# When the second weight slice is fetched and converted, in an attention-then-SwiGLU kernel

## The chip, the core and the metric

One NeuronCore of one Trainium2 chip. The metric is device time in microseconds (us) of one execution. TensorE (PE) multiplies, VectorE (DVE) and ScalarE (ACT) do the elementwise work, and SyncE (SP) issues nearly all DMAs, one after the other in program order.

## The reference

Attention over 4 batches, 12 heads, 448 positions, head size 64, with a sigmoid in place of the softmax, and then a gated feed-forward layer on the 1792 x 768 result:

```python
scores = scale * np.matmul(q, k.transpose(0, 1, 3, 2)) - np.log(S)
attn = 1.0 / (1.0 + np.exp(-scores))
x = np.matmul(attn, v)                       # (4, 12, 448, 64) -> (1792, 768)
xn = x / np.sqrt(np.mean(x * x, axis=-1, keepdims=True) + 1e-06) * rms_g
g = xn @ w_gate                              # 768 x 1536
out = (g * (1.0 / (1.0 + np.exp(-g))) * (xn @ w_val)) @ w_out
```

## The kernel before, in words

The attention runs in 12 units u of four heads; a batch is three units. A unit has 7 steps c. A step is 12 fp16 score matmuls (`scores`, L282, into `sc`), one sigmoid on ACT over 128 x 896 (L286, into one of four `a_b` buffers), and 8 fp32 matmuls with v (`av`, L297). Each fp32 operand of the fp16 products is cut into a high and a low fp16 half.

The loop over `n` (0, 2, ..., 84; called slot n here) walks the 84 steps in pairs: slot n does the scores of steps n and n+1 and then `av` of steps n-2 and n-1. Step 7u + c is step c of unit u, so unit 5 begins at step 35, whose scores are in slot 34 and whose `av` is the second one of slot 36. Unit 6 begins at step 42: scores in slot 42, `av` first in slot 44. Unit 7 begins at step 49 (scores second in slot 48, `av` second in slot 50).

What feeds a unit, in the order of the steps (the table `FILL`, L853): at steps c = 0 to 3 of unit u, DVE splits k and q of unit u+2 (`qk_hi` L227, `qk_lo` L231); behind the last of these, SP issues one transpose DMA (`transpose_both` L234, `xc<-room`) for unit u+2. At c = 4 SP loads k and q of unit u+4. When unit u's last `av` is issued, SP loads v of unit u+2 (`load_v`) into the buffer that unit u has left; there are two v buffers, and a v load is two DMAs of 224 KB. Below, T(u), kq(u) and v(u) are the transpose and the loads of unit u.

Batch results are normalised (`norm`, L340): PE sums squares (`ssq`), DVE computes the inverse root on small tiles, PE spreads it to a row (`rinv`, L392), ACT copies that (L393), DVE scales (L396), adds and subtracts (L403, L418), and the fp16 halves are made (L400 on ACT for batches 0 and 3, L407 on DVE).

The feed-forward layer multiplies by slices of w_gate and w_val of 256 columns each (two-level Strassen products, hence the differences between blocks). A slice of one kind is loaded by three DMAs (`load_w`, L459: one of 384 KB, two of 192 KB) that are put into the list `loads` and go out when `run_load` is called. It is then converted: three DVE steps undo the packing (`to_f32`, L444 to L446), four DVE subtractions form block differences (L496), and ACT and DVE cut the result into fp16 halves (L499, L502). `split_w` returns these steps in two lists: `first` begins with four entries for the gate half (a step that flushes due loads, and the three of `to_f32`, the last of which also puts the next slice's transfers into `loads`), then four for the value half, then the differences; `second` holds the fp16 halves. For slices 0 and 1 the gate and value halves are separate entries.

The steps are not issued at once. `run_later` (L805) is called after every `scores` and every `av`; each call gives a credit of 0.8 for DVE (at most 2.5) and 0.18 for ACT, and takes entries from `adds`, then `norms`, then `splits` as long as the credit is above zero, charging each its cost; `wait` entries let a call pass. The k/q splits are charged too. So what stands in `splits`, and from which slot on, sets where in DVE's in-order stream the other entries come. `SPLIT_AT`, `REST_AT` and `LOADS_AT` (L71, L72) are the slots at whose end entries are put into `splits` and loads are issued. Before the change slice 1's transfers go out one at the end of slot 18, one at 20, two at 26 and two at 28, and all its conversion is put into `splits` at the end of slot 30.

Of the kernel before, what the change touches and what calls it, by code (L numbers as in the profile page):

```python
# [24 lines left out]
def attention_then_swiglu(  # L25
# [42 lines left out]
    ps_m = ctx.enter_context(tc.tile_pool(name="ps_m", bufs=4, space=bass.MemoryType.PSUM))  # L68

    WARM = 5  # L70
    SPLIT_AT, REST_AT = (8, 30), 12  # L71
    LOADS_AT = {18: 1, 20: 1, 26: 2, 28: 2}  # L72
    NAT = (0, 2, 0, 1, 2, 0, 1, 2, 0, 1, 0, 1)
    PIECES = (0, 4), (4, 3)
    K_PIECES = (0, 2), (2, 3), (5, 2)
# [136 lines left out]
    def g_columns():  # L212
        ps = bank("g")
        nc.tensor.matmul(ps[:, :NCC], g_row, ident[:NCC, :NCC], start=True, stop=True)
        nc.vector.tensor_copy(g_sb.rearrange("p (c o) -> p o c", o=2), ps[:, :NCC].rearrange("p (o c) -> p o c", o=2))
# [55 lines left out]
    def scores(u, c):  # L271

        T = t_b[u % 3]
        ps = banks("sc")

        for n, (l, m) in enumerate(PARTS):
            for r in range(2):
                rows = slice(D * r, D * r + D)
                for j in range(2):
                    cols = slice(PB * j, PB * j + PB)  # L280
                    o = ps[cols, r, :S].rearrange("p (c x) -> p c x", c=NSLOT)
                    nc.tensor.matmul(  # L282
                        o, T[rows, 1, l, c, cols], T[rows, 0, m, :, cols], start=(n == 0), stop=(n == 2)
                    )
        a = at[u, c] = a_b[(u * NSLOT + c) % 4]
        nc.scalar.activation(  # L286
            a, ps[:, :, :S], AF.Sigmoid, bias=-math.log(S), scale=1.0 / (math.sqrt(D) * SQ * SQ)
        )

    def av(u, c):  # L290
        a = at.pop((u, c))
        if c == 0:
            pav[u] = [bank("av") for _ in range(2)]
        for r, ps in enumerate(pav[u]):
            for j in range(2):
                rows = slice(PB * j, PB * j + PB)
                nc.tensor.matmul(  # L297
                    ps[D * (j ^ r) : D * (j ^ r) + D, :S],
                    v_b[u % 2][rows, r, c],
                    a[rows, r],  # L300
                    start=(c == 0),
                    stop=(c == NSLOT - 1),
                )
        if c == NSLOT - 1:
            for r, ps in enumerate(pav.pop(u)):
                evict(u, r, ps)
            if u + 2 < NU:
                load_v(u + 2)
# [21 lines left out]
    def run_evictions(n):  # L330
        for part in evictions[:n]:
            part()
        del evictions[:n]
# [132 lines left out]
    def run_load():  # L466
        if loads:
            loads.pop(0)[1]()
# [331 lines left out]
    adds, norms, splits = [], [], []  # L800
# [4 lines left out]
    def run_later():  # L805
        calls[0] += 1
        credit[0] = min(credit[0] + SLOT, 2.5)
        credit[1] = min(credit[1] + ACT_SLOT, 0.6)
        for queue in (adds, norms, splits):
            while queue:  # L810
                part, cost, *on_act = queue[0]
                if part is wait:
                    if cost <= calls[0]:
                        queue.pop(0)
                    break
                if credit[bool(on_act)] <= 0:
                    break
                queue.pop(0)
                part()
                credit[bool(on_act)] -= cost  # L820
# [49 lines left out]
    with tc.manual_schedule():  # L870
# [28 lines left out]
        split = {}  # L899
        for n in range(0, len(todo) + 2, 2):  # L900
            for u, c in todo[n : n + 2]:
                scores(u, c)
                run_evictions(1)
                for part in FILL[c]:
                    part(u)
                if n == 6 and c == 6:
                    g_columns()
                run_later()
            for u, c in todo[max(n - 2, 0) : n]:
                av(u, c)  # L910
                run_evictions(1)
                run_later()
            for _ in range(LOADS_AT.get(n, 0)):
                run_load()
            if n in SPLIT_AT:
                fc = SPLIT_AT.index(n)
                split[fc] = split_w(fc)
                first, second = split[fc]
                splits.extend(first[:4] if fc == 0 else first + second)
            if n == REST_AT:  # L920
                splits.extend(split[0][0][4:] + split[0][1])
        run_evictions(len(evictions))


# [46 lines left out]
        for fc, n in order:  # L971
# [5 lines left out]
            elif fc + 1 < NFC:  # L977
                first, second = split[fc + 1] = split_w(fc + 1) if n == 0 else split[fc + 1]
# [97 lines left out]
```

## Time and profile before

| what | value |
|---|---|
| runs of the kernel | 579.77, 578.42, 576.60 us; median 578.42 |
| the profiled execution | 577.24 us, of which the span is 575.4 |
| PE busy | 562.7 us (98%) |
| DVE busy | 437.9 us (76%) |
| ACT busy | 265.7 us (46%) |
| attention | from the first scores at 8.10 us to about 140 us; then PE works on the feed-forward layer without a gap to the end |

A span row of PE is a share of modelled matmul time; the stretches in which PE has no work are read from the timeline. The timeline merges neighbouring instructions of one kind into a row; in brackets stands the idle time of the engine before the row and what ended it.

### The profile page before, as it was taken

How to read it: one execution, taken by the hardware profiler on the slowest of the kernel's cores; microseconds unless marked ns; L12 is line 12 of the kernel's file. 1: busy time of each engine (PE TensorE's matmuls, PEld its weight loads, DVE VectorE, ACT ScalarE, POOL GpSimd, SP SyncE). 2: the span in 40 equal slices, each digit the busy share in tenths (PEclk: the TensorE clock that was granted, in tenths of full speed). 3: DMA queues.
4: the chain of work that ended last, by engine and by line, in shares of the span. 5: the costliest groups of instructions: out<-in, count | busy, mean ns of one | idle time of the engine just before them, and what ended most of it. 6: DMA issues, size and time to landing. Idle time of an engine off the chain costs nothing.

```text
span 575.4 us, 10231 instructions
## 1 busy us (share of the span) xinstructions
PE 562.7 (98%) x4224; PEld 306.1 (53%) x4224; DVE 437.9 (76%) x577; ACT 265.7 (46%) x398; POOL 0.7 (0%) x6
## 2 busy tenths in 40 slices
PE   8999979999999999999999999999999999999997
PEld 6555435454555555555555555555556566666664
DVE  4897499998887777878778787787557987777751
ACT  5788778887454243342433424334438342222220
POOL 0000000000000000000000000000000000000000
PEclk9999999999999999999999999999999999999999
DMA  8999998972016356282662825732526576444211
GB/s 260 253 217 261 222 255 202 222 168 41 1 43 173 117 158 197 88 227 68 168 190 96 220 78 158 191 104 66 179 59 224 152 224 188 149 145 146 69 41 42
DMA packets 99201, 87.25 MB, mean 152 GB/s; under 512 B 38735, under 2 KB 92242, under 8 KB 99154
## 3 DMA queue, kind: packets, MB, share of 16 engines
q1 hardware_dynamic: 98594, 85.91, 56.7%
q8 instruction: 33, 0.54, 0.4%
q10 hardware_dynamic: 560, 0.69, 0.3%
q14 instruction: 14, 0.11, 0.1%
HBM read 61.34 MB, written 16.52 MB: 135 GB/s over the span
## 4 chain that ended last, share of the span: by engine, by line
PE 90%; DVE 5%; DMA 2%; ACT 1%; issue 1%; SPq 0%; DVEq 0%; ACTq 0%
PE cb L532 28%; PE cd L532 14%; PE av L297 7%; PE oc L735 7%; PE od L735 7%; PE o L735 7%; PE ca L532 7%; PE sc L282 6%; PE ob L735 4%; DMA wr<-in_moe_w_val_dram 1%; DVE room L231 1%; DVE room L396 1%; DVE room L322 1%; ACT room L286 1%; PE tr L251 1%
## 5 line engine op out<-in xcount | busy, mean ns | idle before, releaser
L532 PEld LDWEIGHTS <-wr 128*128 128x128 f16 x1512 | 147.9, 98 | 138.6 <-issue 1.0
L532 PE MATMUL cb<-xc,wr 128*128 128x448 f16 x756 | 147.3, 352 | 0.0
L286 ACT ACTIVATE room<-sc 128x896 f32<-128x896 f32 x84 | 75.1, 930 | 19.5 <-PE sc L282 18.8
L297 PE MATMUL av<-room 64*64 64x448 f32 x672 | 73.7, 538 | 1.4 <-DMA room<-in_v_dram 1.4
L532 PE MATMUL cd<-xc,wr 128*128 128x448 f16 x324 | 65.2, 352 | 0.0
L282 PE MATMUL sc<-xc 64*64 64x448 f16 x1008 | 59.8, 351 | 4.9 <-ACT room L286 4.2
L282 PEld LDWEIGHTS <-xc 64*64 64x64 f16 x1008 | 32.2, 106 | 34.9 <-issue 24.2
L587 DVE TENSOR_TENSOR room<-cd,room 128x448 f32<-128x448 f32 x24 | 15.0, 625 | 43.1 <-PE cd L532 43.1
L735 PEld LDWEIGHTS <-xc 128*128 128x128 f16 x360 | 35.2, 98 | 23.3
L502 DVE SCALAR_TENSOR_TENSOR wr<-wr 128x1536 f16<-128x1536 f32 (+3 forms) x28 | 37.3, 1355 | 10.7 <-ACT wr L499 10.7
L532 PE MATMUL ca<-xc,wr 128*128 128x448 f16 x216 | 44.8, 352 | 0.0
L735 PE MATMUL o<-room,wr 128*128 128x384 f16 x252 | 41.1, 326 | 0.0
L297 PEld LDWEIGHTS av<-room 64*64 64x64 f32 x672 | 27.1, 133 | 24.2 <-issue 16.8
L555 ACT ACTIVATE room<-cb 128x448 f32<-128x448 f32 x24 | 13.0, 543 | 53.8 <-PE cb L532 53.8
L576 ACT ACTIVATE room<-cb 128x448 f32<-128x448 f32 x24 | 13.0, 543 | 50.6 <-PE cb L532 30.6
L735 PEld LDWEIGHTS <-room 128*128 128x128 f16 x270 | 26.4, 98 | 17.5
L499 ACT ACTIVATE wr<-wr 128x768 f16<-128x768 f32 (+1 forms) x48 | 33.9, 758 | 0.0
L590 ACT ACTIVATE room<-room 128x448 f32<-128x448 f32 x24 | 13.8, 577 | 43.2 <-DVE room L587 43.2
L735 PEld LDWEIGHTS <-wr 128*128 128x128 f16 x252 | 24.7, 98 | 16.3
L690 ACT ACTIVATE xc<-xc 128x1536 f16<-128x1536 f32 (+1 forms) x12 | 14.5, 1259 | 35.7 <-DVE xc L687 35.7
L496 DVE TENSOR_TENSOR wr<-wr 128x384 f32<-128x384 f32 x48 | 26.5, 553 | 0.8
L548 ACT ACTIVATE room<-cb 128x448 f32<-128x448 f32 x24 | 13.0, 544 | 25.5 <-PE cb L532 25.5
(98 smaller groups left out, 678.7 us busy)
## 6 DMA issues: line engine op xcount, KB each, us to landing
y_d<-room SPq DMA_DIRECT2D x24, 448.0 KB, 3.3
xc<-in_moe_w_out_dram SPq DMA_DIRECT2D x12, 768.0 KB, 6.1
xc<-y_d SPq DMA_DIRECT2D x22, 384.0 KB, 4.1
room<-in_v_dram SPq DMA_DIRECT2D x24, 224.0 KB, 4.1
out_dram<-room SPq DMA_DIRECT2D x49, 96.0 KB, 2.2
wr<-in_moe_w_gate_dram SPq DMA_DIRECT2D x12, 384.0 KB, 4.2
wr<-in_moe_w_gate_dram SPq DMA_DIRECT2D x24, 192.0 KB, 4.9
wr<-in_moe_w_val_dram SPq DMA_DIRECT2D x12, 384.0 KB, 6.1
```

What stands on the lines that cost most here:

```text
L282: nc.tensor.matmul(o, T[rows, 1, l, c, cols], T[rows, 0, m, :, cols], start=(n == 0), stop=(n == 2))
L286: nc.scalar.activation(a, ps[:, :, :S], AF.Sigmoid, bias=-math.log(S), scale=1.0 / (math.sqrt(D) * SQ * SQ))
L297: nc.tensor.matmul(ps[D * (j ^ r) : D * (j ^ r) + D, :S], v_b[u % 2][rows, r, c], a[rows, r], start=(c == 0), stop=(c == NSLOT - 1),)
L496: first.append((lambda o=o, f0=f0, f1=f1: tt(wf[:, o], wf[:, f0], wf[:, f1], ALU.subtract), 0.6))
L499: nc.scalar.activation(t[:, 0, s], wf[:, s], AF.Copy, scale=SW)
L502: stt(t[:, 1, s], wf[:, s], SW, t[:, 0, s], ALU.mult, ALU.subtract)
L532: nc.tensor.matmul(ps, w[:, l, b, c], xc[n, a][:, r, c], start=(not more and c == 0 and m == 0), stop=(c == NK - 1 and m == 2), skip_group ...
L548: nc.scalar.activation(y[:, 0], pb[:, :S], AF.Copy)
L587: tt(y[:, 1], pd[:, :S], y[:, 1], ALU.add)
L590: nc.scalar.activation(y[:, 1], y[:, 1], AF.Silu, scale=UNIT)
L690: return lambda: nc.scalar.activation(s[:, 0, a:b], f[:, a:b], AF.Copy), 0.0, ()
L735: nc.tensor.matmul(ps[:, :HALF], a(m, l), w(m, r), start=(not more and m == 0 and n == 0), stop=(m == NM - 1 and n == 2), skip_group_check ...
```

## The change

Two tables of slots change, and the way in which slice 1's conversion is put into `splits`. Slice 1's three gate transfers all go out at slots 18 (one) and 20 (two), its three value transfers together at the end of slot 28, that is behind v(5), which the `av` of the same slot has issued. At slot 30 only the gate half (`first[:4]`) is put into `splits`; the value half, the differences and the fp16 halves follow at slot 36. Slice 0 is treated as before (slots 8 and 12), with the code written for both slices.

```diff
-    SPLIT_AT, REST_AT = (8, 30), 12
-    LOADS_AT = {18: 1, 20: 1, 26: 2, 28: 2}
+    SPLIT_AT, REST_AT = (8, 30), (12, 36)
+    LOADS_AT = {18: 1, 20: 2, 28: 3}
...
                 fc = SPLIT_AT.index(n)
                 split[fc] = split_w(fc)
                 first, second = split[fc]
-                splits.extend(first[:4] if fc == 0 else first + second)
-            if n == REST_AT:
-                splits.extend(split[0][0][4:] + split[0][1])
+                splits.extend(first[:4])
+            if n in REST_AT:
+                first, second = split[REST_AT.index(n)]
+                splits.extend(first[4:] + second)
```

## Rows read from the trace of the kernel before

**Rows 1.** Busy times by stretch; columns PE, PEld, DVE, ACT, POOL, granted clock, DMA share, GB/s
```profile
56.00:92.00 36.00, 30.14 (x414) 15.92 (x410) 27.72 (x40) 27.44 (x42) 0.00 (x0) 1.00 1.02 230
92.00:143.00 51.00, 50.63 (x706) 25.48 (x699) 48.17 (x76) 41.95 (x62) 0.00 (x0) 1.00 0.74 159
```

**Rows 2.** The chain that ended last, 56 to 99 us; columns start, length, what
```profile
61.98 6.26 DMA wr<-in_moe_w_val_dram
...
89.87 0.95 PE ssq L354 x8
...
97.13 0.49 PE rinv L392 x2
```

**Rows 3.** Timeline of DVE, 56 to 87 us
```profile
63.04 0.56 DVE L444 TENSOR_SCALAR wr<-wr 128x768 uint32<-128x768 uint32 x1 [5.83 <-DMA wr<-in_moe_w_gate_dram]
...
68.36 0.56 DVE L444 TENSOR_SCALAR wr<-wr 128x768 uint32<-128x768 uint32 x1 [2.24 <-DMA wr<-in_moe_w_val_dram]
...
73.45 1.55 DVE L396 TENSOR_TENSOR room<-room 128x1344 f32<-128x1344 f32 x1
...
85.25 1.15 DVE L231 SCALAR_TENSOR_TENSOR room<-xc,room 128x448 f16<-128x448 f32 x2
```

**Rows 4.** Timeline of ACT, its longest wait between 56 and 99 us
```profile
75.03 1.04 ACT L400 ACTIVATE xc<-room 128x448 f16<-128x448 f32 x2 [3.08 <-DVE room L396]
```

**Rows 5.** Timeline of PE, 55 to 104 us
```profile
55.82 1.68 PE L297 MATMUL av<-room 64*64 64x448 f32 x16
...
63.22 1.30 PE L282 MATMUL sc<-xc 64*64 64x448 f16 x24
...
66.20 0.97 PE L297 MATMUL av<-room 64*64 64x448 f32 x4 [0.92 <-DMA room<-in_v_dram]
...
76.93 1.57 PE L282 MATMUL sc<-xc 64*64 64x448 f16 x24 [3.05 <-ACT room L286]
...
80.94 1.70 PE L297 MATMUL av<-room 64*64 64x448 f32 x16
...
99.64 1.30 PE L282 MATMUL sc<-xc 64*64 64x448 f16 x24
...
102.28 1.30 PE L282 MATMUL sc<-xc 64*64 64x448 f16 x24
```

**Rows 6.** Timeline of SP, 38 to 81 us: its DMA issues
```profile
38.60 5.76 SPq L234 DMA_TRANSPOSE xc<-room  x1
...
46.46 1.11 SPq L464 DMA_DIRECT2D wr<-in_moe_w_gate_dram  x2
47.67 1.94 SPq L190 DMA_DIRECT2D room<-in_v_dram  x2
49.71 6.04 SPq L234 DMA_TRANSPOSE xc<-room  x1
...
58.59 0.63 SPq L464 DMA_DIRECT2D wr<-in_moe_w_gate_dram  x1
...
59.99 0.87 SPq L190 DMA_DIRECT2D room<-in_v_dram  x2
60.91 1.69 SPq L464 DMA_DIRECT2D wr<-in_moe_w_val_dram  x2
62.71 8.05 SPq L234 DMA_TRANSPOSE xc<-room  x1
...
72.90 0.85 SPq L190 DMA_DIRECT2D room<-in_v_dram  x2
76.10 4.27 SPq L234 DMA_TRANSPOSE xc<-room  x1
```

**Rows 7.** DMA issues of 62.7 to 73.9 us; last column: us to landing
```profile
room<-in_v_dram SPq DMA_DIRECT2D x2, 224.0 KB, 4.5
xc<-room SPq DMA_TRANSPOSE x1, 9.9
```

**Rows 8.** The same for the issues of 46.4 to 47.6 us
```profile
wr<-in_moe_w_gate_dram SPq DMA_DIRECT2D x1, 192.0 KB, 6.6
```

## The prediction
> **What bounds the kernel now.** Read first the busy times by stretch: PE stands idle for 5.86 us of 56 to 92 us and for 0.37 us of the 51 us behind it, at a granted clock of 1.00 in both [rows 1]. Everything that can be won in attention lies in this one stretch, and the reader is to ask what held PE there. The chain of waits names a value transfer, 6.26 us long, landing at 68.24 [rows 2]. DVE's timeline shows what it did: DVE ran dry at 57.21 (63.04 less 5.83), waited for the last gate transfer, and then 2.24 us for the last value transfer, in all 8.07 us [rows 3]. Everything behind in its in-order stream came late: the second norm scaling ends at 75.0, ACT waited 3.08 us for it in its own stream, and PE had its longest gap, 3.05 us, at slot 42 (76.93) waiting for ACT [rows 3 to 5]. A second gap is of another kind: at slot 36 the `av` of unit 5 waits for v(5) (0.92 us until 66.20, with a shorter wait for the second half) [rows 5]. SP's timeline says why: v(5) is free to go once the `av` of slot 28 is done, some 55 us, but T(5) holds SP from 49.71 to 55.75, and kq(7), a gate and a value transfer stand ahead of v(5), which goes at 59.99 [rows 6].
>
> How far PE is from its floor: where nothing waits a slot takes 102.28 - 99.64 = 2.64 us, and a norm's `ssq` and `rinv` take about 0.9 and 0.5 [rows 2, 5]. From slot 36 (63.22) to slot 56 (99.64) ten slots and one norm should take 26.4 + 1.4 = 27.8 us; they took 36.4. So 8.6 us is the ceiling of any gain; the difference from the idle time is matmuls that the profile draws out.
>
> **The change, part by part.** No instruction is added or removed; six transfers and some DVE and ACT steps change places. I count in the code which call of `run_later` issues which entry (credit 0.8, the costs in the lists).
>
> *Transfers at slots 18 and 20.* `loads` is filled by then (the gate step of slice 0 is charged at slot 10, the value step at 14), so the move does happen. One 192 KB gate transfer, 0.63 us of SP, leaves its place behind kq(7) and goes ahead of v(4) and T(5), which go 0.6 us later. v(4) is needed at 55.82 in slot 30 [rows 5]. Its landing is not shown. The 192 KB transfer ahead of it landed at about 53.6 (46.98 + 6.6) [rows 6, 8], so v(4) lies between 54.5 and 55.8 and the move costs PE between 0 and 0.7 us there. I take 0, since a later wait would swallow it (below).
>
> *Gate conversion at slot 30.* All gate transfers then are issued before 48.5; with the 6.6 us shown they land before 55.2, ahead of 57.21. The wait of 5.83 us goes whole [rows 3, 6, 8].
>
> *v(5) ahead of the values.* The first value transfer, 0.77 us of SP (59.22 to 59.99), moves behind v(5), and 384 KB no longer lie ahead of it in the queue. Bounds for v(5): as late as now, or earlier by 0.77 us and by 384 KB at the stretch's 230 GB/s, 1.67 us more. I take 2 us, near the second end; the wait of slot 36 goes.
>
> *T(6) and v(6): what is late next.* SP does the same work ahead of T(6) as before, in another order, so T(6) starts at 62.7 again, takes 8.05 us behind the same bytes and lands 9.9 us after its start, at 72.6 [rows 6, 7]. Without waits PE wants it in slot 42, at 63.22 + 3 x 2.64 = 71.1: a new wait of 1.5 us. Then kq(8), and v(6) at 72.90, landing 4.5 us on, 77.4; PE wants it at 72.6 + 2.64 + 1.1 = 76.4: a further 1.0 us. Before, this `av` of slot 44 ran at 80.94 [rows 5]. **Gain up to there 80.94 - 77.4 = 3.5 us**, whatever v(4), v(5) or ACT lose of the 2.5 us of waits ahead of it. Bounds: 2.7 to 4.4 us, with the two landings 0.9 us later or earlier.
>
> *From slot 44 to 56.* Before 99.64 - 80.94 = 18.70 us; the floor is 1.5 + 5 x 2.64 + 1.4 = 16.1. The excess is 2.6 us; bounds of what goes: 0 to 2.6. It came of the backlog that ACT and DVE had gathered by 75 us [rows 3, 4]. ACT's norm halves now are issued in slots 38 to 42 and run while PE waits for T(6) and v(6). I take 0.8 us as what stays: **gain 1.8 us more**.
>
> *DVE, which must keep up.* It is nearly full until 143 us (48.17 of 51) [rows 1], so PE can't win more than DVE does. From 63.04 to the end of the split for T(8), 86.4 (85.25 + 1.15), DVE's work with the 2.24 us wait out is 21.1 us [rows 3]. My count puts the same entries there plus one 1.5 us subtraction less one of 0.5, so 22.1 from 57.21, plus about 1 us waiting for kq(7) and the norm row: 80.4. DVE comes to the first value step at about 68.4, just as the values land (68.24), because the norm's three passes now stand ahead. DVE's lead of 6.0 us covers the gain; if that step waited long, the lead shrinks by as much. From slot 48 on, my count gives the same order as before, and one norm entry left at the end as before, so the feed-forward part only shifts.
>
> *Sum.* 3.5 + 1.8 = 5.3 us off the profiled execution's 577.24 (span 575.4 and 1.84 around it): 571.9. The median, 578.42, lies 1.18 above that execution: **573.1 us**.
>
> On T(6) a figure stands against my landing time. Rows 2 and 7 show T(6) landing 4.4 us after the last value transfer (72.6 against 68.24). The Trainium skill (DMA: Bandwidth & Descriptors, Latency and other measured facts) gives a DMA transpose 261 GB/s in the non-contiguous case. For the 917 KB of one unit (128 partitions of 7,168 bytes) my estimate from it is 3.5 us, 0.9 us less than the trace; by it the sum would be 0.9 us larger, 572.2.
>
> **The rivals.**
> - *The transpose chain is shorter.* With loads reordered, T(6) might clear 0.9 us sooner (the early bound above), and kq(8) and v(6) with it: gain 4.4 + 1.8, 572.2. For it: SP took only 4.27 us for T(7) [rows 6]. Against: the same bytes stand ahead of T(6). The skill's figure above would give this.
> - *SP's chain becomes the pace for one more unit.* T(7) waited for DVE until 76.10; now its split is done by 68.4 and it goes at once behind v(6), at 73.8, into a full queue. If it takes T(6)'s 8.05 us rather than 4.27, kq(9) goes at 81.9 and DVE, coming to its split about 82.8, waits some 3 us for it, which leaves 3.0 us of DVE's lead: 578.4 - 3.0 = 575.4. For it: T(4) to T(6) took 5.76 to 8.05 us each behind loads [rows 6]. Against: no weight transfers are ahead of T(7).
> - *Given back on DVE.* If the values land late, DVE stands at the first value step with the splits for unit 8 behind it; at 74 us the lead of 6.0 us is gone and the time is 578. For it: they still leave at about 60.2, right ahead of a transpose. Against: the last landed at 68.24 with the same bytes ahead.
> - *Slower: the queue falls behind unit after unit.* From T(5) to T(6) a unit took SP 62.71 - 49.71 = 13.0 us; from T(4) to T(5) 11.1, with 576 KB of weights [rows 6]. If units 7 to 9 each took 13.0 from v(6) on, v(9) would land at 77.4 + 39 = 116.4, where slot 64 wants it at about 112 now: 4 us slower, 582. It decides above 11.5 us a unit, (112 - 77.4)/3. Against: the 13.0 held 960 KB of weights; at 1.9 us per 384 KB (13.0 against 11.1) a unit without them takes 8.3, less than PE's 9.2.
>
> **How the numbers follow.** The forecast 0.48 (571.3 to 574.7 by its bounds), shorter chain 0.07, SP's chain 0.19, given back 0.16, slower 0.10. A measurement of this kernel tells 0.5%, 2.9 us, from no change, so faster means under 575.5. Forecast, shorter chain and nearly all of SP's chain lie there: 0.73; given back and the rest 0.17; slower 0.10. The range from 570.0 (the early bound with all 2.6 us of the excess gone, 571.4, and the spread of the runs, 1.4) to 577.0 takes in SP's chain and the milder half of given back.
>
> **What would show it.** In the changed profile: no DVE wait for a gate transfer, and one under 1 us for a value transfer at about 68; no PE wait for v(5); the scores of slot 42 at about 72.6 behind T(6), and the `av` of slot 44 at about 77.4 behind v(6); T(7) issued at about 74; slot 56 at about 94.3; feed-forward rows shifted by about 5 us and otherwise alike. It is wrong if T(6) lands after 74, if DVE waits over 2 us at the value step or for kq(9), or if slots 46 to 56 still take 2 us over their floor.

## The result, and the profile after

The changed kernel takes 572.75 us (median of 9 runs; the kernel before 577.59 beside it), a ratio of 0.9915 with a 95% interval of 0.9888 to 0.9942. One of the nine, 593.73 us at a mean granted clock of 0.949, is a slow run that the ratio leaves out; the median of the other eight is 572.55. The forecast was 573.1. The profiled execution takes 572.34 us (571.9 forecast) with a span of 570.5, 4.9 less than before. The first product of the feed-forward layer starts at 135.00 us against 139.89: the whole 4.9 us are won in attention, and what follows is only shifted.

Busy times by stretch, in the columns of rows 1:

```profile
56.00:92.00 36.00, 33.82 (x472) 18.61 (x464) 31.51 (x55) 31.23 (x48) 0.00 (x0) 1.00 1.12 238
92.00:143.00 51.00, 50.60 (x667) 25.20 (x660) 47.98 (x74) 38.45 (x57) 0.00 (x0) 1.00 0.71 152
```

PE's idle time in the first stretch fell from 5.86 to 2.18 us [rows 1], and DVE does 3.8 us more work there. The timeline of DVE:

```profile
56.31 0.56 DVE L444 TENSOR_SCALAR wr<-wr 128x768 uint32<-128x768 uint32 x1
...
60.88 0.63 DVE L227 TENSOR_SCALAR room<-xc 128x896 f16<-128x896 f32 x1 [1.49 <-DMA xc<-in_k_dram]
...
63.96 1.55 DVE L396 TENSOR_TENSOR room<-room 128x1344 f32<-128x1344 f32 x1
...
68.51 0.55 DVE L444 TENSOR_SCALAR wr<-wr 128x768 uint32<-128x768 uint32 x1
...
79.38 1.15 DVE L231 SCALAR_TENSOR_TENSOR room<-xc,room 128x448 f16<-128x448 f32 x2
```

Both waits for weights are gone: the gate half begins at 56.31, the value half at 68.51, neither with a wait in brackets. The second norm scaling ends at 65.5 instead of 75.0, and the split for T(8) at 80.5 instead of 86.4, a lead of 5.9 us [rows 3]. ACT finds its input ready (its L400 runs at 68.00 without the wait of rows 4). The timeline of PE:

```profile
62.79 1.30 PE L282 MATMUL sc<-xc 64*64 64x448 f16 x24
...
69.90 0.76 PE L282 MATMUL sc<-xc 64*64 64x448 f16 x12 [0.61 <-ACT room L286]
70.47 1.70 PE L297 MATMUL av<-room 64*64 64x448 f32 x16
72.31 1.33 PE L282 MATMUL sc<-xc 64*64 64x448 f16 x24
...
77.71 2.03 PE L297 MATMUL av<-room 64*64 64x448 f32 x14 [1.43 <-DMA room<-in_v_dram]
...
86.20 1.33 PE L282 MATMUL sc<-xc 64*64 64x448 f16 x24
...
94.75 1.30 PE L282 MATMUL sc<-xc 64*64 64x448 f16 x24
```

The gaps of 0.92 us (v(5), slot 36) and 3.05 us (ACT, slot 42) are gone [rows 5]. In their place stand a short wait for ACT in slot 40 and one of 1.43 us for v(6) in slot 44. SP, and the landing of T(6) in the last column of the second fence:

```profile
45.19 1.76 SPq L464 DMA_DIRECT2D wr<-in_moe_w_gate_dram  x3
47.05 1.47 SPq L190 DMA_DIRECT2D room<-in_v_dram  x2
48.62 7.65 SPq L234 DMA_TRANSPOSE xc<-room  x1
...
59.25 0.85 SPq L190 DMA_DIRECT2D room<-in_v_dram  x2
60.14 2.17 SPq L464 DMA_DIRECT2D wr<-in_moe_w_val_dram  x3
62.42 7.88 SPq L234 DMA_TRANSPOSE xc<-room  x1
...
72.45 0.85 SPq L190 DMA_DIRECT2D room<-in_v_dram  x2
73.39 6.14 SPq L234 DMA_TRANSPOSE xc<-room  x1
```

```profile
xc<-room SPq DMA_TRANSPOSE x1, 9.8
```

T(6) starts at 62.42 (62.71 before), holds SP for 7.88 us and lands at 72.2 (62.42 + 9.8); v(6) leaves at 72.45 (72.90) [rows 6, 7]. That chain stands where it stood, and PE has moved up to it.

### The profile page after: what moved, and what is told of

It is laid out like the page before. It is cut to its first block, busy times and chain, and to the rows that moved or that the text cites. A ratio compares the mean times of both kernels' runs of the same rounds, so it can differ in the third digit from the quotient of the medians.

```text
span 570.5 us, 10232 instructions
## 1 busy us (share of the span) xinstructions
PE 561.1 (98%) x4224; PEld 305.2 (54%) x4224; DVE 437.8 (77%) x577; ACT 265.6 (47%) x398; POOL 0.7 (0%) x6
## 4 chain that ended last, share of the span: by engine, by line
PE 90%; DVE 4%; DMA 3%; ACT 1%; SPq 1%; issue 1%; ACTq 0%; DVEq 0%
PE cb L532 28%; PE cd L532 14%; PE av L297 8%; PE oc L735 7%; PE o L735 7%; PE od L735 7%; PE ca L532 7%; PE sc L282 6%; PE ob L735 4%; DVE room L396 1%; DMA room<-in_v_dram 1%; DMA room<-in_q_dram 1%; DMA xc<-in_k_dram 1%; SPq L190 1%; ACT room L286 1%; PE ssq L354 1%
## 5 line engine op out<-in xcount | busy, mean ns | idle before, releaser
L286 ACT ACTIVATE room<-sc 128x896 f32<-128x896 f32 x84 | 75.2, 929 | 18.4 <-PE sc L282 17.7
L282 PE MATMUL sc<-xc 64*64 64x448 f16 x1008 | 59.9, 351 | 1.7 <-ACT room L286 1.0
L282 PEld LDWEIGHTS <-xc 64*64 64x64 f16 x1008 | 32.5, 106 | 30.9 <-issue 19.0
```

The lines of the kernel that those rows point to most:

```text
L282: nc.tensor.matmul(o, T[rows, 1, l, c, cols], T[rows, 0, m, :, cols], start=(n == 0), stop=(n == 2))
L286: nc.scalar.activation(a, ps[:, :, :S], AF.Sigmoid, bias=-math.log(S), scale=1.0 / (math.sqrt(D) * SQ * SQ))
```

## The experiments

Theory: what cost was DVE standing in its in-order stream at a conversion whose transfer had not landed; with that gone, the queue's chain of T(6), v(6) and T(7) is the bound. Rivals: the order of the transfers alone; ACT's blocked stream alone; SP's in-order issue. In the table stands the time from the scores of slot 36 to those of slot 50 (floor 19.4 us: seven slots of 2.64 and one `ssq`), from there to the first feed-forward product, and DVE's longest wait for a weight transfer, all from the profiles.

| kernel | median us | ratio to before (95%) | 36 to 50 | 50 to first product | DVE wait |
|---|---|---|---|---|---|
| before | 577.6 | 1 | 27.5 | 49.1 | 5.8 and 2.2 |
| the change | 572.75 | 0.9915 (0.9888 to 0.9942) | 23.4 | 48.8 | none |
| e1 loads only | 577.73 | 1.0001 (0.9985 to 1.0016) | 28.7 | 48.8 | 8.7 |
| e2 conversion only | 575.02 | 0.9954 (0.9935 to 0.9973) | 26.6 | 49.1 | 7.8 |
| e3 values ahead of v(5) | 573.53 | 0.9927 (0.9905 to 0.995) | 21.8 | 49.1 | none |
| e4 kq(8) behind v(6) | 573.65 | 0.9927 (0.9905 to 0.9949) | 22.4 | 49.5 | none |
| e5 values behind T(7) | 585.15 | 1.012 (1.0096 to 1.0145) | 20.5 | 57.9 | 6.3 |
| e6 values behind v(6) | 577.34 | 0.9994 (0.9977 to 1.0011) | 23.2 | 51.4 | 1.8 |
| e7 v from POOL | 573.84 | 0.993 (0.9909 to 0.9952) | 20.5 | 49.1 | none |
| e8 before, halves on DVE | 582.16 | 1.0074 (1.0055 to 1.0094) | 28.7 | 52.1 | 6.5 and 1.4 |
| e9 no value transfers | 570.34 | 0.9873 (0.984 to 0.9907) | 20.5 | 49.1 | none |
| e10 before, no slice 1 | 570.18 | 0.9866 (0.9834 to 0.9898) | 21.2 | 48.8 | none |
| e11 values split | 578.06 | 0.9998 (0.9972 to 1.0024) | 25.8 | 51.7 | 4.1 |

Waits are not all that these columns hold. In some of the profiles the granted clock fell to 0.50 behind a PE gap: in e1 and e2 between slots 36 and 50, in e5, e8 and e11 in slot 50, in e6 and once more in e5 after the first product, in e7 ahead of slot 36. What it cost stands with the runs.

**e1, the loads alone.** `LOADS_AT` as changed, conversion as before:

```diff
-    SPLIT_AT, REST_AT = (8, 30), (12, 36)
+    SPLIT_AT, REST_AT = (8, 30), (12,)
...
-                splits.extend(first[:4])
+                splits.extend(first[:4] if fc == 0 else first + second)
```

> The new load slots, but all of slice 1's conversion put into splits at slot 30 as before. Theory (the gain needs DVE free of the value wait): DVE converts the gate half at about 56.5 without a wait, then stands about 8 us at the value half until the values land near 68; its lead over the kernel before is under 1 us, and the time is 576.8 (576 to 577.6). Rival (the order of the transfers, v(5) ahead of the values, brings the gain): about 573.

Measured 577.73, no difference from before. The timelines of DVE and of PE, and the busy times of a stretch behind PE's gap, in the columns of rows 1 (the granted clock is the third number from the right):

```profile
68.61 0.56 DVE L444 TENSOR_SCALAR wr<-wr 128x768 uint32<-128x768 uint32 x1 [8.68 <-DMA wr<-in_moe_w_val_dram]
```

```profile
77.18 2.45 PE L282 MATMUL sc<-xc 64*64 64x448 f16 x24 [5.77 <-ACT room L286]
```

```profile
78.00:80.00 2.00, 2.00 (x24) 1.14 (x20) 1.93 (x4) 1.58 (x3) 0.00 (x0) 0.50 1.17 215
```

The two waits of before have become one of 8.68 us, PE's small gaps at slot 36 (0.92 and 0.46) went and the one at slot 42 grew from 3.05 to 5.77, so slot 42 begins no earlier. In that gap the granted clock fell to 0.50, and slot 42 took 4.77 us (77.18 to 81.95) instead of 2.64. So of the 5.3 us by which slots 36 to 50 are longer than in the change, 2.1 are the clock's; the rest is PE waiting behind DVE. The rival is out: the order of the transfers alone wins nothing.

**e2, the conversion alone.** `LOADS_AT` as before, the rest as changed.

```diff
-    LOADS_AT = {18: 1, 20: 2, 28: 3}
+    LOADS_AT = {18: 1, 20: 1, 26: 2, 28: 2}
```

> The loads at the slots of before, the value half put into splits at slot 36. Theory: the 5.8 us wait for the last gate transfer stays and DVE's lead is only some 1.3 us, so PE gains at slot 42 and loses most of it again by slot 50: 576.2 (575 to 577). Rival (moving the value half alone brings the gain): about 573. v(5)'s wait of slot 36 stays, under both.

Measured 575.02, 1.2 us better than the theory's value and at the edge of its range. The wait for the gate stays, longer than before:

```profile
65.34 0.56 DVE L444 TENSOR_SCALAR wr<-wr 128x768 uint32<-128x768 uint32 x1 [7.83 <-DMA wr<-in_moe_w_gate_dram]
```

but DVE's second wait is gone, and the norm's scaling comes ahead of the value half. PE's wait for v(5) stays (1.13 us). This is roughly half of the gain. Its rival, all of the gain, lies outside the interval. Part of what is missing is the clock's, which fell behind PE's longest gap; the row of the gap, and the busy times behind it:

```profile
74.90 1.33 PE L282 MATMUL sc<-xc 64*64 64x448 f16 x12 [2.70 <-ACT room L286]
```

```profile
75.00:78.00 3.00, 3.00 (x24) 1.45 (x27) 2.96 (x6) 3.00 (x6) 0.00 (x0) 0.50 0.90 257
```

From this row to slot 42 (78.59) it took 3.69 us, where e9, below, takes 2.07 (68.92 to 70.99): 1.6 us. The profiled execution of e2 is the slowest of its seven runs, so its column in the table is on the long side.

**e3, v(5) behind the values.**

```diff
-    LOADS_AT = {18: 1, 20: 2, 28: 3}
+    LOADS_AT = {18: 1, 20: 2, 26: 3}
```

> The changed kernel with all three value transfers ahead of v(5) (slot 26), so that v(5) lands some 3 us later. Theory (T(6), v(6) and ACT's lag end the stretch later anyway, about 2.5 us of waits swallow it): PE waits about 3 us for v(5) in slot 36, the av of slot 44 comes at about 78, and the time is within 1 us of the changed kernel, 573.2. Rival (v(5)'s place in the queue is what counts): 3 us slower than the change, 576.

Measured 573.53, not to be told from the change, as the theory had it. But the wait for v(5) is not 3 us:

```profile
65.79 1.24 PE L297 MATMUL av<-room 64*64 64x448 f32 x6 [0.37 <-DMA room<-in_v_dram]
```

SP issued the values at 57.08 and v(5) at 60.05 here, against 59.99 before, with 768 KB of weights right ahead of it and not 576 (192 of the gate, 384 of the values), and PE's wait for it ended no later (65.79 against 66.20). So the bytes ahead of v(5) did not set its landing as the prediction took them to. v(5)'s place is worth 0.4 us of wait here, and no time that these runs can tell.

One more thing stands in this profile: PE waits for neither T(6) nor v(6). T(6) held SP for 5.96 us from 61.56, v(6) left at 70.44, 2 us earlier than in the change with the same bytes moved, and slots 36 to 50 took 21.8 us instead of 23.4. This execution is the fastest of its six, and the median is no better than the change's, so a gain is not shown. But the landings of T(6) and v(6) are not fixed by the bytes ahead of them.

**e4, v(6) ahead of kq(8).** In `av`, behind the load of v(6), and left out of its old place:

```diff
             if u + 2 < NU:
                 load_v(u + 2)
+            if u == 4:
+                load_qk(8, K)
+                load_qk(8, Q)
```

> The changed kernel with kq(8) issued behind v(6) instead of ahead of it. Theory (v(6)'s landing is the bound left at slot 44): v(6) goes at 70.4 and lands near 75, PE's wait of 1.4 us at slot 44 goes, DVE waits about 2 us for kq(8) instead of 0.5; the time is 571.7 (1 us less than the change). Rival (T(6) or DVE is the bound): 572.7 or more, with slot 56 where it was.

Measured 573.65. The wait for v(6) is gone as expected, and one transfer later another has come (L286 is L282 of the others here):

```profile
82.14 0.76 PE L286 MATMUL sc<-xc 64*64 64x448 f16 x12 [1.30 <-DMA xc<-room]
```

That is T(7), which left at 72.74 behind kq(8) and lands 9.4 us later. The theory that v(6) alone is the bound failed: this reordering handed the wait on to the next transfer of the chain.

**e5, e6, e11, the values later.** The gate step no longer flushes them; then

```diff
-    SPLIT_AT, REST_AT = (8, 30), (12, 36)
-    LOADS_AT = {18: 1, 20: 2, 28: 3}
+    ... e5:  (12, 46)   {18: 1, 20: 2, 40: 3}
+    ... e6:  (12, 42)   {18: 1, 20: 2, 36: 3}
+    ... e11: (12, 40)   {18: 1, 20: 2, 28: 1, 36: 2}
```

> The changed kernel with the three value transfers not at slot 28 but at slot 40, behind T(7) and kq(9), and the value half put into splits at slot 46 (the gate step no longer flushes them). Theory (the waits left in slots 42 to 48 are the queue's, which carries 768 KB too much ahead of T(6), v(6) and T(7)): T(6) starts near 60.2 and lands near 69, v(6) near 73, no PE wait in slots 42 and 44, at most 0.5 us at units 7 and 8, slot 56 near 93; 571.4. Rival (slice 1's later DVE steps push four norm entries behind slot 84, ahead of the first feed-forward products, and cost there what is won): 573 or more.

> The changed kernel with the three value transfers at the end of slot 36, right behind v(6) and ahead of T(7), the value half put into splits at slot 42. Theory (the queue's total is the bound, and what is taken from ahead of one unit's transfers stands ahead of the next one's): no PE wait in slots 42 and 44, but T(7) lands near 81.5 and PE waits about 2 us for it in slot 48; 572.9, as the changed kernel. Rival (only unit 6 was tight): 571.

> The changed kernel with the first value transfer at slot 28 behind v(5), the other two at slot 36 behind v(6), and the value half put into splits at slot 40 (as many norm entries left at the end as in the changed kernel). Theory (the queue's total up to T(7) is what ends last): v(6) about 1 us earlier, PE's wait at slot 44 under 0.5 us, T(7) no earlier, so 0.5 to 1 us won by slot 50 if DVE waits under 2 us for the last value transfer; 572.3, not to be told from the changed kernel. Rival (v(6) alone is the bound left): 571.

e5 shows both of its theories at work: no PE wait for a transfer at units 6 and 7 (slot 50 comes 20.5 us after slot 36, 2.9 us sooner than in the change), and then 9.1 us lost up to the first product. DVE met the value half at 79 us, waited 6.3 us for the transfers that had left at 77.76, and PE stood 4.62 us in slot 50, with the clock at 0.50 behind it; the norm entries left over cost the feed-forward part another 3.2 us of idle PE (43.84 of the 47 us from 143 to 190). e6 has the wait for T(7) that the theory gave it:

```profile
83.09 0.76 PE L282 MATMUL sc<-xc 64*64 64x448 f16 x12 [2.36 <-DMA xc<-room]
```

with slot 50 as late as in the change. It is still 4.6 us slower than the change, which the expectation did not foresee. Two places of the loss are named by the trace: 2.6 us go between slot 50 and the first product, where a v load is late once more (0.22 us at 108.24, with the slots behind it drawn out), and here too the left-over norm entries make PE wait in the feed-forward part (2.06 us at 146.06 for `rinv`, and the clock fell to 0.50 behind it). e11 is the cleanest. No PE wait for T(6), v(6) or T(7) is left in it, and no left-over norm entry more than in the change. One DVE wait remains, and it undoes everything:

```profile
76.69 0.56 DVE L444 TENSOR_SCALAR wr<-wr 128x768 uint32<-128x768 uint32 x1 [4.14 <-DMA wr<-in_moe_w_val_dram]
```

```profile
86.76 1.39 PE L354 MATMUL ssq<-ones,room 128*112 128x1 f32 x8 [4.71 <-DVE room L322]
88.08 2.46 PE L282 MATMUL sc<-xc 64*64 64x448 f16 x24
```

4.14 us on DVE became 4.71 us on PE, because `ssq` needs a sum that stands behind the conversion in DVE's stream; then the clock fell again (slot 50 took 5.2 us, 88.08 to 93.30, instead of 2.64). My 2 us for that wait was the miss in its expectation.

**e7, v from POOL.** `load` takes the issuing engine as a new argument (not shown); the call:

```diff
-        load(v, v_b[u % 2], u)
+        load(v, v_b[u % 2], u, nc.gpsimd if u > 1 else None)
```

> The changed kernel with v(2) to v(11) issued from POOL instead of SP, so that they don't stand behind SP's transposes. Theory (the bytes and the transposes, not SP's order, set the landings): v(5) and v(6) go at 55 and 65 and PE's wait for v(6) goes, but T(6) and T(7) land later by as much; within 1.5 us of the changed kernel, 572.9. Rival (SP's in-order issue is the bound): 570.5 to 571.2.

Measured 573.84, within the theory's bound. With v no longer behind SP's transposes, slots 36 to 50 take 20.5 us without a wait for v, but they start at 66.87: T(5) held SP for 9.43 us and PE waited for it,

```profile
63.09 1.15 PE L282 MATMUL sc<-xc 64*64 64x448 f16 x12 [2.61 <-DMA xc<-room]
```

Here too the clock fell behind the gap:

```profile
64.00:66.00 2.00, 2.00 (x16) 0.74 (x12) 1.76 (x2) 0.92 (x1) 0.00 (x0) 0.50 1.09 333
```

From 63.09 to slot 36 (66.87) it took 3.78 us instead of 2.07, so 1.7 us of the late start are the clock's. Yet the three of the six runs with a mean clock of 0.999 or 1.0 took 572.19, 572.97 and 573.55 us, no less than the change, so the rival fails without this loss too: SP's in-order issue is not what sets the remaining 2 to 3 us. That the bytes to be moved set them is what e9 speaks for, below.

**e8, ACT out of the way.** In the kernel before:

```diff
-            if b in (1, 2):
+            if b < 3:
```

> The kernel before, with batch 0's fp16 high halves made on DVE (as for batches 1 and 2) instead of ACT, so that ACT has nothing in its stream that waits for DVE's late norm steps. Theory (DVE being late is the bound, and ACT only the first to hand it on): PE's 3.05 us gap for ACT at slot 42 goes, but T(7), whose split DVE still ends near 76, lands near 84, and PE waits some 4 us in slot 48; 577.6, as the kernel before. Rival (ACT's blocked stream is what cost): 574.5.

Measured 582.16, slower than both theories. The gap at slot 42 is gone, as expected, but no wait for T(7) came. ACT now waits for DVE elsewhere, where a new square must not overwrite the last one before DVE has added it:

```profile
77.32 0.54 ACT L316 ACTIVATE room<-av 128x448 f32<-128x448 f32 x1 [2.10 <-DVE room L322]
...
82.63 0.54 ACT L316 ACTIVATE xc<-av 128x448 f32<-128x448 f32 x1 [2.63 <-DVE room L322]
```

PE stood 2.24 us (for ACT, until 84.56) and 2.18 us (for DVE, until 89.81); the clock then fell to 0.50, and slot 50 took 5.23 us (91.24 to 96.47), which is 2.6 us of the loss. DVE, already late, also has two casts of 0.85 us more, so this run does not test ACT's part by itself. What it shows is that PE's gap doesn't need ACT's norm steps: as long as DVE is late, ACT and PE wait for it elsewhere.

**e9 and e10, no transfers.** e9 is the changed kernel without slice 1's three value transfers, e10 the kernel before without all six; the halves are converted from what slice 0 left in the buffers, with the same steps.

```diff
+        if (fc, kind) == (1, 1):          # e10: if fc == 1
+            loads.extend([(1, wait)] * 3)
+            return
```

> The changed kernel without slice 1's three value transfers (its value half is converted from what slice 0 left in the buffer); the order of everything else is kept. Theory (the waits that are left in slots 42 to 48 are the price of 768 KB in a full queue): T(6) starts near 60.2, no PE wait for T(6), v(6) or T(7), slot 50 near 83.5 and slot 56 near 92; 570 (2.5 to 3 us under the changed kernel). Rival (ACT's and DVE's own work hold PE there anyway): 572.

> The kernel before without slice 1's six transfers (its halves are converted from what slice 0 left), conversion in the old order, all from slot 30 on. Theory (DVE's wait for transfers is the whole cost, not the order of its entries): no DVE wait from 57 on but for kq(7) and the norm's row, no PE gap at slot 42, 570 as the changed kernel without values. Rival (the six conversion steps ahead of the norm's scaling themselves hold ACT and PE up): 572 to 574.

570.34 and 570.18: both theories' values, and the same for both orders, though e10 leaves out the gate's transfers too. In e9 PE's only wait in slots 36 to 50 is the 0.61 us for ACT; in e10, with all conversion from slot 30 on as before, slots 36 to 50 take 21.2 us against 27.5. So the old order of DVE's entries costs little in itself (0.7 us more than e9 in the profiles, nothing in the medians). It cost because a transfer was late in it.

## Why the prediction was right, point by point

*The wait for the gate transfers goes whole:* yes, 5.83 to 0. *The value step comes just as the values land:* DVE reached it at 68.51 (68.4 forecast), 0.7 us after the last value transfer had landed, and did not wait. e1, e5 and e11, each with 4 to 9 us of such a wait, show that this is the point on which the change turns.

*T(6) and v(6) stay where they were and end the stretch next:* T(6) landed at 72.2 (72.6), slot 42 began at 72.31, the `av` of slot 44 at 77.71 (77.4). The first term is 80.94 - 77.71 = 3.2 us for 3.5 [rows 5]. 0.43 of it was there ahead of slot 36 already (62.79 for 63.22), where the profiles of the other kernels, e7 apart, scatter from 62.29 to 63.83; it isn't put down to the change. The landings came as forecast, but the wait for T(6) did not: of 1.5 us PE's matmuls show 0.14 (72.17 to 72.31) and the weight loads ahead of them 0.9:

```profile
PEld L282 <- DMA xc<-room: 0.9, 1, 0.9
```

Slots 36 to 40 had taken 9.4 us instead of the floor's 7.9, in part by 0.61 us of waiting for ACT, which the forecast did not have. The wait for v(6) was 1.43 us for 1.0.

There is luck in the landings too. The forecast took it that T(6) would hold SP for 8.05 us again, behind the same bytes; it was 7.88. With slice 1's weights all ahead of it, it was 8.07 in e1, 6.83 in e4, 6.70 in e2 and 5.96 in e3.

*Excess from slot 44 to 56:* 94.75 - 77.71 = 17.0 against a floor of 16.1, so 0.9 us stayed where 0.8 was taken; the second term is 1.7 for 1.8.

*DVE's lead* of 5.9 us (6.0) covered the gain.

*The sum:* 4.9 us off the profiled execution for 5.3. The median came closer to the forecast than that, since the 578.42 that it starts from was the median of three runs; the nine have 577.59.

*v(5):* mis-sized. It did leave 0.74 us earlier and PE's matmuls did not wait (their weight loads 0.3 us), but e3 took away both advantages and lost 0.37 us of wait. It did not enter the sum.

*The rivals.* A shorter transpose chain did not come in the change, but e3's profile shows that it can. T(7) left at 73.39 and held SP for 6.14 us, between the 4.27 and 8.05 of the second bullet's two cases; kq(9) left at 79.58 and DVE's split from it, at 84.69, did not wait. T(6) landed 4.4 us after the values did (the last left at 61.7 and landed 6.1 us on, T(6) at 72.2), as before. By the prediction's estimate from the Trainium skill's rate for a transpose (DMA: Bandwidth & Descriptors, Latency and other measured facts) it would have landed 0.9 us sooner; the trace differs from that rate as it did before. The queue did not fall behind unit after unit: T(6) to T(7) and T(7) to T(8) took SP 11.0 and 9.2 us.

What stays open: the change still pays some 2.4 us for the values' 768 KB (572.75 against 570.34 in e9; the intervals overlap a little, so the size is not settled), and none of e3 to e7 and e11 found a place for them that is cheaper. No kernel that does the whole computation was faster than the change.

## What to carry to other kernels

A step that converts a transferred tile belongs in an in-order engine's stream behind everything that others wait for and that could run before the transfer lands; ask at which time the engine will reach it, not only at which time the transfer leaves. Moving transfers in a full queue hands the wait to the next transfer (v(6) to T(7) in e4, v(6) to T(5) in e7); what wins is taking the wait off the engine that has no slack. And a wait costs more than its length where the granted clock falls behind the gap that it opens in front of TensorE: 1.6 us more in e2, 2.6 in e11.

## What the runs showed of the hardware that was not expected

The granted clock fell to 0.50, the lower of the two levels (1.2 against 2.4 GHz), in or behind PE gaps of 5.77 us (e1), 4.71 us (e11) and 4.62 us (e5), and stayed there for 4 to 7 us of work; 24 score matmuls took 2.45 us instead of 1.3. The length of the gap alone does not settle it: the clock also fell behind gaps of 2.70 us (e2), 2.61 us (e7), 2.94 us (e5, 150.82), 2.06 us (e6) and the two of 2.24 and 2.18 us in e8, while behind the 3.05 us gap in the profile of the kernel before it stood at 1.00. Yet over 18 runs of that kernel beside e1 the mean clock was 0.994 to 0.999, against 0.998 to 1.0 over eight runs of the change. So in many runs of the kernel before some clock was lost that its one profile does not show, and the gap at slot 42 is the likely place, which is not shown. It is the smaller part of the gain: the three runs of the kernel before, beside the experiments, that show a mean clock of 0.999 took 577.09, 577.42 and 577.03 us, and the two profiles, with no fall of the clock in attention, differ by 4.9 us.
